# A linear attention with two feed-forward layers: a shorter bit algorithm for float64 weights, spread out phase by phase, and limb subtractions on VectorE

## The chip, the cores and the metric

The program runs on one core of a Trainium2 chip. Its engines work side by side, each through its own list of instructions in order: TensorE (PE), VectorE (DVE), ScalarE (ACT), GpSimd (POOL) and SyncE (SP), which issues the transfers. The metric is the device time in microseconds (us) of one execution, as the median of several runs; lower is better.

## What is computed

Three stages, float32 in and out, over 4 batches x 576 tokens (2304 in all), 8 heads of 64:

```python
q_p, k_p = phi(q * scale), phi(k * scale)      # phi: exp(x omega^T - |x|^2/2 - max), 128 features
num = q_p @ (k_p^T v);  den = q_p @ sum(k_p)   # linear attention, per batch and head
x = num / (den + 1e-6)                         # 2304 x 512
h = x @ moe_w_in;  g = relu(h) ** 2;  x = g @ moe_w_out      # 512 -> 2048 -> 512
h = x @ moe2_w_in; g = elu(h);        out = g @ moe2_w_out
```

The four weight matrices arrive as float64. The kernel makes float32 of them by operations on their bits.

## The kernel before

**Precision.** Every float32 operand of the large products is split into two limbs, high and low (`h`, `l`): ACT writes the high one with a cast, and a subtraction, the helper `minus` (line 74), leaves the low one. A product then is three matmuls (high x high, high x low, low x high) that accumulate in a PSUM bank.

**Attention.** The work is cut into 36 units: per batch four of k, four of q and one of the tokens left over. They pass through a hand-written list of stages (lines 516 to 519), one unit further per *tick*: load, square (POOL), transpose on PE with cast (ACT, `th`) and subtraction (DVE, `tl`), projection on PE (`pp`), maxima (DVE), exp (ACT), use on PE, division (DVE, `xs`), transpose again with limbs (`xh`, `xl`). `tc.manual_schedule()` keeps this order: what is issued first in a tick stands first in its engine's list. From tick 16 on, a tick also holds one or two products of the feed-forward layers.

**Feed-forward layers.** Per layer 16 chunks f of 128 columns of the hidden dimension, in 4 groups of 4. In a group the five token blocks (four of 512 tokens, a small one of 256) are worked on in turn, the small one second, but last in the last group. A *step* is a block and a chunk: `gemm1`, 12 matmuls, with the activation behind it (`r`, `gf`, its limbs `gh` and `gl`), and two steps later `gemm2`, 12 matmuls into `py`. After a block's fourth step DVE adds the banks to `ya` (lines 478 to 485). So PE alternates gemm1 of a step and gemm2 of the step two before; each is called a product below. All PSUM is a pool of 8 banks, all large data a pool of 93 pages.

**Weights.** A matrix chunk (a *part*, 64 in all) goes through three phases: `make_squares` (fetch, and a Square of the high words on ACT, tile `cm`), `make_floats` (four bit operations on DVE, tile `cv`), `make_limbs` (cast `wh` on ACT, subtraction `wl` on POOL). Three staging buffers (`st`) hold fetched chunks. `make(n)` takes one part each through all three phases, oldest first. It is called in each tick from 13 on for the first group's 8 parts, and after attention on every second product, up to 12 parts ahead of the number already used up.

Of the kernel before, what the change touches and what calls it, by code (L numbers as in the profile page):

```python
# [17 lines left out]
def linear_attention_two_ffn_kernel(  # L18
# [19 lines left out]
    C = S // P                    # whole token tiles of a batch  # L38
    L = S - C * P                 # tokens left over
    LH = 2                        # of the tokens left over, heads on top of each other on the partitions  # L40
    KD = DM // P
    NF = DFF // P
    GF = 4                        # f chunks of a group
    NG = NF // GF
    BLKS = [C * P] * B + [B * L]  # token blocks: the whole tiles of each batch, then what is left
    NB = len(BLKS)
    W = 512
    LOOK = 2                      # steps from a gemm1 to its gemm2
# [3 lines left out]
    # the square of the float32 that has a float64's high word for 2^-126 as its bits  # L52
    TINY = (1.125 * 2.0 ** -15) ** 2
# [5 lines left out]
    # nearly all data lives in pages of one size  # L59
# [19 lines left out]
    # x of each layer and block, d on the partitions: pages of limbs, one a chunk of d (two for the small block)  # L79
    xh, xl = {}, {}  # L80

    def x_pages(moe, i, c, name):
        """pages of chunk c, and their part for it"""
        per = W // BLKS[i]
        for d, s in ((xh, "h"), (xl, "l")):
            if (moe, i, c // per) not in d:
                d[moe, i, c // per] = page([per, BLKS[i]], f"x{s}{moe}_{i}_{c // per}", F32R)

# [26 lines left out]
    # Keeps sign and the exponent's top bit, drops the three exponent bits that float32 has not, and takes  # L115
    # three mantissa bits of the low word; what float32 holds no normal number for goes to zero.
    def make_squares(n):
# [3 lines left out]
        nc.scalar.activation(out=staged[p][1], in_=staged[p][0][:, :, 1].bitcast(F32), func=AF.Square)  # L121

    def make_floats(n):
# [4 lines left out]
        nc.vector.tensor_scalar(  # L128
            out=t, in0=hi, scalar1=3, scalar2=0x3FFFFFFF, op0=ALU.logical_shift_left, op1=ALU.bitwise_and
        )  # L130
        nc.vector.scalar_tensor_tensor(  # L131
            out=t, in0=hi, scalar=0xC0000000, in1=t, op0=ALU.bitwise_and, op1=ALU.bitwise_or
        )
# [3 lines left out]
        tf = t.bitcast(F32)  # L137
        nc.vector.scalar_tensor_tensor(out=tf, in0=m, scalar=TINY, in1=tf, op0=ALU.is_ge, op1=ALU.mult)  # L138
        staged[p] = tf
        fetch(n + 3)  # L140

    def make_limbs(n):
# [5 lines left out]
        minus(nc.gpsimd, l, tf, h)  # L148
        w_t[p] = h, l

    def make(n):
        """goes on with the parts before n, each one phase further"""
        n = min(n, len(parts))
        for f, c in ((make_limbs, 2), (make_floats, 1), (make_squares, 0)):
            if n_made[c] < (n if c == 0 else n_made[c - 1]):
                f(n_made[c])
# [8 lines left out]
    # A unit is [P, 4, 2, D]: four pairs of rows of D, each pair of one partition's tokens (or, of the tokens  # L165
    # left over, of two heads). A pair is transposed and projected as one, by a block diagonal omega^T.
# [43 lines left out]
    def load_v(u):  # L210
# [4 lines left out]
        if kind == "l":  # L215
            # of two heads on top of each other, each with zeros beside it
# [20 lines left out]
    def transposed(u):  # L237
        """x^T of a unit, scaled, in limbs; the sum over d of x^2"""
# [29 lines left out]
    def maxima(u):  # L268
# [9 lines left out]
        # max h = max(proj) - sq / 2;  h - max h = proj - sq / 2 - max h  # L278
# [3 lines left out]
    def featured(u):  # L282
        """exp(h - max h) of a unit, token by token"""
# [12 lines left out]
    def used(u):  # L296
        """phi(k)^T [v, 1] of two heads, or phi(q)^T of a unit"""
# [227 lines left out]
    with tc.manual_schedule():  # L525
        load(units[0])
        omega_limbs()
        for s in range(1, len(units) + DEPTH):
            for f, d in stages:
# [3 lines left out]
                elif f == "weights":  # L533
                    if s >= WEIGHTS:
                        make(2 * GF)
# [38 lines left out]
```

## Time and profile before

| | before |
|---|---|
| device time, median of 3 runs (lowest to highest) | 1016.61 us (1015.27 to 1016.76) |
| span of the profiled execution, first to last instruction | 1009.8 us |
| median of the runs above that span | 6.8 us |
| PE busy | 978.4 us, 97% |
| DVE busy | 637.0 us, 63% |
| ACT busy | 476.3 us, 47% |
| POOL busy | 391.8 us, 39% |
| mean granted TensorE clock | 0.992 of full speed (2.4 GHz) |

Attention fills the first quarter of the span, layer 1 (moe=0) the time up to about 600 us, layer 2 (moe=1) the rest. The busy share is an average over these: which engine is waited for is a question to each stretch. A busy time counts an instruction from its start to its modelled end; matmuls overlap, so their rate is read from the number that start in a stretch (x in the tables by stage).

### The profile page before, as it was taken

What the parts mean: (1) busy time and instruction counts of PE and PEld (TensorE: products, weight loads), DVE (VectorE), ACT (ScalarE), POOL (GpSimd) and SP (SyncE); (2) the same over time, 40 slices, a digit from 0 to 9 for tenths busy, and PEclk for the clock granted to TensorE, in tenths of its full rate; (3) what the DMA queues carried; (4) which work ended last, traced back from release to release, by engine and by line L of the source; (5) the groups of instructions that cost most, each with busy time, mean ns of one, the idle gap of its engine ahead of it and who ended that gap; (6) DMA issues with size and microseconds to landing.
All of it is one profiled execution on the core that took longest, in us unless ns stands there. A gap on an engine that the chain in (4) does not pass through costs nothing.

```text
span 1009.8 us, 14294 instructions
## 1 busy us (share of the span) xinstructions
PE 978.4 (97%) x5441; PEld 840.7 (83%) x5441; DVE 637.0 (63%) x1031; ACT 476.3 (47%) x1051; POOL 391.8 (39%) x359
## 2 busy tenths in 40 slices
PE   8977999999999999999999997999999999999998
PEld 7977899999888888888888886888788878888886
DVE  7899866654797249524962498339933993384333
ACT  6875565654443234322443354445454545454443
POOL 7345533321445225423464465224522443243221
PEclk9998999999999999999999999999999999999999
DMA  7333421200222002100210022002200230000211
GB/s 180 115 115 105 114 50 48 74 2 2 82 89 80 1 21 84 63 1 21 87 61 0 8 80 81 1 1 83 84 1 1 67 100 1 1 21 1 78 48 63
DMA packets 56469, 53.39 MB, mean 53 GB/s; under 512 B 25424, under 2 KB 50000, under 8 KB 56400
## 3 DMA queue, kind: packets, MB, share of 16 engines
q1 hardware_dynamic: 56240, 52.21, 17.0%
q8 instruction: 43, 0.70, 0.3%
q10 hardware_dynamic: 160, 0.26, 0.1%
q14 instruction: 26, 0.21, 0.1%
HBM read 47.74 MB, written 4.72 MB: 52 GB/s over the span
## 4 chain that ended last, share of the span: by engine, by line
PE 76%; DVE 19%; issue 2%; ACT 1%; DMA 1%; SPq 0%; POOL 0%; DVEq 0%; POOLq 0%; ACTq 0%
PE ph L419 33%; PE py L461 32%; DVE cv L134 4%; DVE cv L138 3%; DVE cv L131 3%; PE pn L345 2%; DVE cv L128 2%; DVE r L439 1%; DVE ya L485 1%; DVE gf L440 1%; PE pk2k L312 1%; PE pk3k L312 1%; PE pk0k L312 1%; PE pp2q L263 1%; PE pp3k L263 1%
## 5 line engine op out<-in xcount | busy, mean ns | idle before, releaser
L74 POOL TENSOR_TENSOR gl<-gf,gh 128x512 fp32r<-128x512 f32 (+1 forms) x171 | 195.0, 1141 | 569.0 <-ACT gh L441 241.3
L419 PE MATMUL ph<-xh,wh 128*128 128x512 f32 (+1 forms) x688 | 246.5, 358 | 5.5 <-DVE gf L440 5.5
L419 PE MATMUL ph<-xl,wh 128*128 128x512 f32 (+1 forms) x688 | 246.1, 358 | 0.0
L419 PE MATMUL ph<-xh,wl 128*128 128x512 f32 (+1 forms) x688 | 246.1, 358 | 0.0
L419 PEld LDWEIGHTS ph<-xh,wh 128*128 128x128 f32 x688 | 129.9, 189 | 27.8 <-DVE gf L440 6.8
L439 DVE SCALAR_TENSOR_TENSOR r<-r,t 128x512 f32<-128x512 f32 (+1 forms) x80 | 52.7, 658 | 158.8 <-ACT t L438 158.8
L432 DVE TENSOR_TENSOR gf<-r 128x512 f32<-128x512 f32 (+1 forms) x92 | 55.5, 604 | 151.7 <-ACT r L430 150.8
L419 PEld LDWEIGHTS ph<-xl,wh 128*128 128x128 f32 x688 | 129.7, 189 | 21.0
L419 PEld LDWEIGHTS ph<-xh,wl 128*128 128x128 f32 x688 | 129.7, 188 | 20.6
L430 ACT ACTIVATE r<-ph 128x512 f32<-128x512 f32 (+1 forms) x92 | 46.5, 506 | 211.6 <-PE ph L419 209.1
L461 PE MATMUL py<-gh,wh 128*128 128x512 f32 (+1 forms) x368 | 128.6, 349 | 0.0
L461 PE MATMUL py<-gl,wh 128*128 128x512 f32 (+1 forms) x368 | 127.0, 345 | 0.0
L461 PE MATMUL py<-gh,wl 128*128 128x512 f32 (+1 forms) x368 | 126.9, 345 | 0.0
L461 PE MATMUL py<-wh,gl 128*128 128x512 f32 x288 | 114.7, 398 | 2.4 <-POOL gl L74 2.4
L441 ACT CAST gh<-gf 128x512 fp32r<-128x512 f32 (+1 forms) x80 | 46.2, 578 | 148.8 <-DVE gf L440 148.8
L461 PE MATMUL py<-wh,gh 128*128 128x512 f32 x288 | 114.2, 396 | 1.3 <-ACT gh L441 1.3
L461 PE MATMUL py<-wl,gh 128*128 128x512 f32 x288 | 113.9, 395 | 0.0
L74 POOL TENSOR_TENSOR wl<-cv,wh 128x512 fp32r<-128x512 f32 x64 | 103.3, 1613 | 26.6 <-ACT wh L147 26.4
L134 DVE SCALAR_TENSOR_TENSOR cv<-st,cv 128x512 uint32<-128x512 uint32 x64 | 88.7, 1386 | 2.2
L461 PEld LDWEIGHTS py<-gh,wh 128*128 128x128 f32 x368 | 69.2, 188 | 9.5
L461 PEld LDWEIGHTS py<-gh,wl 128*128 128x128 f32 x368 | 69.3, 188 | 9.3
L461 PEld LDWEIGHTS py<-gl,wh 128*128 128x128 f32 x368 | 69.2, 188 | 9.3
(322 smaller groups left out, 1600.4 us busy)
## 6 DMA issues: line engine op xcount, KB each, us to landing
st<-in_moe_w_in_dram SPq DMA_DIRECT2D x32, 512.0 KB, 3.6
st<-in_moe_w_out_dram SPq DMA_DIRECT2D x32, 512.0 KB, 3.4
out_dram<-ya SPq DMA_DIRECT2D x16, 256.0 KB, 2.3
ld0k<-in_k_dram SPq DMA_DIRECT2D x4, 256.0 KB, 3.6
v0k<-in_v_dram SPq DMA_DIRECT2D x8, 128.0 KB, 4.2
ld0q<-in_q_dram SPq DMA_DIRECT2D x4, 256.0 KB, 3.8
ld1k<-in_k_dram SPq DMA_DIRECT2D x4, 256.0 KB, 4.9
v1k<-in_v_dram SPq DMA_DIRECT2D x8, 128.0 KB, 3.9
```

Source lines behind the costliest of these rows:

```text
L74: eng.tensor_tensor(out=out, in0=whole, in1=hi.bitcast(F32), op=ALU.subtract)
L128: nc.vector.tensor_scalar(out=t, in0=hi, scalar1=3, scalar2=0x3FFFFFFF, op0=ALU.logical_shift_left, op1=ALU.bitwise_and)
L131: nc.vector.scalar_tensor_tensor(out=t, in0=hi, scalar=0xC0000000, in1=t, op0=ALU.bitwise_and, op1=ALU.bitwise_or)
L134: nc.vector.scalar_tensor_tensor(out=t, in0=lo, scalar=29, in1=t, op0=ALU.logical_shift_right, op1=ALU.bitwise_or)
L138: nc.vector.scalar_tensor_tensor(out=tf, in0=m, scalar=TINY, in1=tf, op0=ALU.is_ge, op1=ALU.mult)
L312: nc.tensor.matmul(o, phs[h][:, c, :], st[u]["v"][:, h * C + c, :], start=False, stop=c == C - 1, skip_group_check=True,)
L419: nc.tensor.matmul(ph[:, :n], wt[:, cs], x_part(xt, moe, i, c)[:, n0:n1], start=(m == 0), stop=(m == 3 * KD - 1))
L430: nc.scalar.activation(out=r, in_=ph[:, :n], func=AF.Relu)
L432: nc.vector.tensor_tensor(out=gf, in0=r, in1=r, op=ALU.mult)
L439: nc.vector.scalar_tensor_tensor(out=r, in0=r, scalar=1.0, in1=t, op0=ALU.add, op1=ALU.mult)
L441: nc.scalar.copy(out=gh, in_=gf)
L461: nc.tensor.matmul(y, *((w[:, ts], a) if moe == 0 else (a[:, ts], w)), start=j == 0 and m == 0 and t % per == 0, stop=j == GF - 1 and m == ...
```

## The change

- The conversion's bit algorithm: ACT multiplies the high words, read as float32, by 2^-112 instead of squaring them; DVE then builds the float32 with one mask and two shift-and-or operations, three instructions instead of four.
- `make` takes the phases that it is to go on with. In attention one phase per tick from tick 2 on (a part per three ticks), after it one phase per product (a part per three products), instead of all three in each tick from 13 on and on every second product.
- Every `minus` runs on DVE: `wl` of the weights, `gl` of the activations, `xl` of layer 2's input, which ran on POOL.

```diff
-    def make_squares(n):
+    def make_rebiased(n):
         fetch(n + 1)
         p = parts[n]
         staged[p] = staged[p], page([W], "cm{}_{}_{}".format(*p))
-        nc.scalar.activation(out=staged[p][1], in_=staged[p][0][:, :, 1].bitcast(F32), func=AF.Square)
+        nc.scalar.activation(out=staged[p][1], in_=staged[p][0][:, :, 1].bitcast(F32), func=AF.Copy, scale=REBIAS)
 
     def make_floats(n):
...
-        nc.vector.tensor_scalar(
-            out=t, in0=hi, scalar1=3, scalar2=0x3FFFFFFF, op0=ALU.logical_shift_left, op1=ALU.bitwise_and
-        )
-        nc.vector.scalar_tensor_tensor(
-            out=t, in0=hi, scalar=0xC0000000, in1=t, op0=ALU.bitwise_and, op1=ALU.bitwise_or
-        )
+        nc.vector.tensor_scalar(out=t, in0=hi, scalar1=0x80000000, scalar2=None, op0=ALU.bitwise_and)
         nc.vector.scalar_tensor_tensor(
             out=t, in0=lo, scalar=29, in1=t, op0=ALU.logical_shift_right, op1=ALU.bitwise_or
         )
-        tf = t.bitcast(F32)
-        nc.vector.scalar_tensor_tensor(out=tf, in0=m, scalar=TINY, in1=tf, op0=ALU.is_ge, op1=ALU.mult)
-        staged[p] = tf
+        nc.vector.scalar_tensor_tensor(
+            out=t, in0=m.bitcast(U32), scalar=3, in1=t, op0=ALU.logical_shift_left, op1=ALU.bitwise_or
+        )
+        staged[p] = t.bitcast(F32)
         fetch(n + 3)
 
     def make_limbs(n):
...
         nc.scalar.copy(out=h, in_=tf)
-        minus(nc.gpsimd, l, tf, h)
+        minus(nc.vector, l, tf, h)
         w_t[p] = h, l
 
-    def make(n):
-        """goes on with the parts before n, each one phase further"""
+    def make(n, phases=(2, 1, 0)):
         n = min(n, len(parts))
-        for f, c in ((make_limbs, 2), (make_floats, 1), (make_squares, 0)):
+        for c in phases:
             if n_made[c] < (n if c == 0 else n_made[c - 1]):
-                f(n_made[c])
+                (make_rebiased, make_floats, make_limbs)[c](n_made[c])
                 n_made[c] += 1
...
-        minus(nc.vector if (moe, g, o, j) == steps[-1] else nc.gpsimd, gl, gf, gh)
+        minus(nc.vector, gl, gf, gh)
...
-                minus(nc.gpsimd, lo, ya, hi)
+                minus(nc.vector, lo, ya, hi)
...
-    WEIGHTS, TWO = 13, 25
+    WEIGHTS, TWO = 2, 25
...
                     if s >= WEIGHTS:
-                        make(2 * GF)
+                        make(2 * GF, ((s - WEIGHTS) % 3,))
...
         for n, s in enumerate(work):
-            if n % 2 == 0:
-                make(n_dead[0] + 12)
+            make(n_dead[0] + 12, (2 - n % 3,))
```

Three places show how the instructions move. The first is the start of ACT's list, ticks 1 to 4. `th0k`, `th0l` and `th0q` are the casts of the first three units, `cm_0_0` and `wh_0_0` belong to the first part of the weights, `st_0_0` is its staging buffer. Before:

```order
L249 ACT_TABLE_LOAD
L249 CAST th0k_114<-pt0k_109 128x512
L249 CAST th0l_136<-pt0l_131 128x512
L249 CAST th0q_172<-pt0q_167 128x512
L290 ACTIVATE ph0k_0_176<-pp0k_0_140,nb0k_157 128x128 x4
```

With the change:

```order
L122 ACT_TABLE_LOAD
L122 ACTIVATE cm_0_0_106<-st_0_0_104 128x512
L246 CAST th0k_118<-pt0k_113 128x512
L246 CAST th0l_148<-pt0l_143 128x512
L144 CAST wh_0_0_174<-cv_0_0_130 128x512
L246 CAST th0q_188<-pt0q_183 128x512
```

`cm_0_0`, which reads a fetched chunk of the weights, now stands ahead of the first unit's cast, and `wh_0_0` ahead of the third's.

The second is DVE's list at the turn to layer 2: `ya0_3_0` to `ya0_3_3` are the last block's sums of layer 1 (their limbs `xh1_3`, `xl1_3` are layer 2's input), `r1_0_0_0_2`, `gf` and `gl` belong to layer 2's third step, `wl1_3_0` is the low limb of the weights of its fourth. Before (`xl1_3`, `gl` and `wl1_3_0` are on POOL, `wl1_3_0` ahead of the four `xl1_3`):

```order
L440 TENSOR_TENSOR gf1_0_0_0_1_6664<-r1_0_0_0_1_6667,ph1_0_0_0_1_6651 128x512
L485 TENSOR_TENSOR ya0_3_0_4034<-py0_3_3_0_0_6526,ya0_3_0_4034 128x512
L485 TENSOR_TENSOR ya0_3_1_4036<-py0_3_3_0_1_6527,ya0_3_1_4036 128x512
L485 TENSOR_TENSOR ya0_3_2_4038<-py0_3_3_0_2_6528,ya0_3_2_4038 128x512
L485 TENSOR_TENSOR ya0_3_3_4040<-py0_3_3_0_3_6529,ya0_3_3_4040 128x512
L128 TENSOR_SCALAR cv1_4_0_6712<-st1_4_0_6597 128x512
L131 SCALAR_TENSOR_TENSOR cv1_4_0_6712<-st1_4_0_6597,cv1_4_0_6712 128x512
L134 SCALAR_TENSOR_TENSOR cv1_4_0_6712<-st1_4_0_6597,cv1_4_0_6712 128x512
L138 SCALAR_TENSOR_TENSOR cv1_4_0_6712<-cm1_4_0_6649,cv1_4_0_6712 128x512
L439 SCALAR_TENSOR_TENSOR r1_0_0_0_2_6737<-r1_0_0_0_2_6737,t1_0_0_0_2_6738 128x512
L440 TENSOR_TENSOR gf1_0_0_0_2_6734<-r1_0_0_0_2_6737,ph1_0_0_0_2_6721 128x512
```

With the change:

```order
L482 TENSOR_TENSOR ya0_3_0_4006<-py0_3_3_0_0_6487,ya0_3_0_4006 128x512
L74 TENSOR_TENSOR xl1_3_0_6636<-ya0_3_0_4006,xh1_3_0_6635 128x512
L482 TENSOR_TENSOR ya0_3_1_4008<-py0_3_3_0_1_6488,ya0_3_1_4008 128x512
L74 TENSOR_TENSOR xl1_3_1_6641<-ya0_3_1_4008,xh1_3_1_6640 128x512
L482 TENSOR_TENSOR ya0_3_2_4010<-py0_3_3_0_2_6489,ya0_3_2_4010 128x512
L74 TENSOR_TENSOR xl1_3_2_6646<-ya0_3_2_4010,xh1_3_2_6645 128x512
L482 TENSOR_TENSOR ya0_3_3_4012<-py0_3_3_0_3_6490,ya0_3_3_4012 128x512
L74 TENSOR_TENSOR xl1_3_3_6651<-ya0_3_3_4012,xh1_3_3_6650 128x512
L436 SCALAR_TENSOR_TENSOR r1_0_0_0_2_6672<-r1_0_0_0_2_6672,t1_0_0_0_2_6673 128x512
L437 TENSOR_TENSOR gf1_0_0_0_2_6669<-r1_0_0_0_2_6672,ph1_0_0_0_2_6656 128x512
L74 TENSOR_TENSOR gl1_0_0_0_2_6671<-gf1_0_0_0_2_6669,gh1_0_0_0_2_6670 128x512
L74 TENSOR_TENSOR wl1_3_0_6682<-cv1_3_0_6616,wh1_3_0_6681 128x512
```

Each `xl1_3` now stands between two `ya0_3` on DVE, and `wl1_3_0` comes behind all of them and behind the third step's `gl`; before, DVE was converting the next group's first part (`cv1_4_0`) there.

The third is DVE's list in layer 1's second group: `gf0_1_0_0_2` is of the step with block 0 and the third chunk, `wl0_6_1`, `cv0_7_0` and `wl0_7_0` are of the weights of the third and fourth chunk. Before:

```order
L128 TENSOR_SCALAR cv0_8_0_4232<-st0_8_0_4141 128x512
L131 SCALAR_TENSOR_TENSOR cv0_8_0_4232<-st0_8_0_4141,cv0_8_0_4232 128x512
L134 SCALAR_TENSOR_TENSOR cv0_8_0_4232<-st0_8_0_4141,cv0_8_0_4232 128x512
L138 SCALAR_TENSOR_TENSOR cv0_8_0_4232<-cm0_8_0_4189,cv0_8_0_4232 128x512
L432 TENSOR_TENSOR gf0_1_0_0_2_4254<-r0_1_0_0_2_4257 128x512
L128 TENSOR_SCALAR cv0_8_1_4282<-st0_8_1_4187 128x512
L131 SCALAR_TENSOR_TENSOR cv0_8_1_4282<-st0_8_1_4187,cv0_8_1_4282 128x512
L134 SCALAR_TENSOR_TENSOR cv0_8_1_4282<-st0_8_1_4187,cv0_8_1_4282 128x512
L138 SCALAR_TENSOR_TENSOR cv0_8_1_4282<-cm0_8_1_4239,cv0_8_1_4282 128x512
L432 TENSOR_TENSOR gf0_1_0_0_3_4304<-r0_1_0_0_3_4307 128x512
```

With the change:

```order
L429 TENSOR_TENSOR gf0_1_0_0_2_4201<-r0_1_0_0_2_4204 128x512
L74 TENSOR_TENSOR gl0_1_0_0_2_4203<-gf0_1_0_0_2_4201,gh0_1_0_0_2_4202 128x512
L74 TENSOR_TENSOR wl0_6_1_4210<-cv0_6_1_4164,wh0_6_1_4209 128x512
L129 TENSOR_SCALAR cv0_7_0_4229<-st0_7_0_4102 128x512
L130 SCALAR_TENSOR_TENSOR cv0_7_0_4229<-st0_7_0_4102,cv0_7_0_4229 128x512
L133 SCALAR_TENSOR_TENSOR cv0_7_0_4229<-cm0_7_0_4186,cv0_7_0_4229 128x512
L74 TENSOR_TENSOR wl0_7_0_4236<-cv0_7_0_4229,wh0_7_0_4235 128x512
L429 TENSOR_TENSOR gf0_1_0_0_3_4252<-r0_1_0_0_3_4255 128x512
L74 TENSOR_TENSOR gl0_1_0_0_3_4254<-gf0_1_0_0_3_4252,gh0_1_0_0_3_4253 128x512
```

Where DVE converted the third group's first part (`cv0_8_0`, `cv0_8_1`) around this step, it now converts `cv0_7_0`, and its `wl0_7_0` follows at once: the next product on PE after the running one, gemm1 of the fourth chunk, reads it.

## Rows read from the trace of the kernel before

**Rows 1.** The page: busy time and share of PE, and its 40 slices.

```profile
PE 978.4 (97%) x5441; PEld 840.7 (83%) x5441; DVE 637.0 (63%) x1031; ACT 476.3 (47%) x1051; POOL 391.8 (39%) x359
PE   8977999999999999999999997999999999999998
```

**Rows 2.** The chain of waits: start, length, engine, tile, line, count.

```profile
251.94 2.78 PE ph L419 x12
```

**Rows 3.** By stage: length, busy PE, PEld, DVE, ACT, POOL (instructions), clock, DMA, GB/s.

```profile
0.00:25.00 25.00, 20.31 (x142) 18.72 (x142) 19.71 (x38) 15.30 (x44) 18.27 (x32) 1.00 0.70 179
15.00:50.00 35.00, 35.00 (x313) 34.68 (x312) 31.64 (x78) 28.90 (x94) 18.18 (x27) 1.00 0.56 154
25.00:50.00 25.00, 25.00 (x226) 24.81 (x225) 21.85 (x61) 20.00 (x66) 8.57 (x15) 1.00 0.39 119
50.00:111.00 61.00, 48.55 (x375) 46.28 (x373) 58.81 (x110) 39.43 (x113) 29.66 (x32) 0.92 0.34 101
```

**Rows 4.** The same table for tile cv alone: DVE, ACT, POOL.

```profile
50.00:111.00 61.00, 30.28 (x32) 5.01 (x8) 10.12 (x8) 0.92 0.34 101
```

**Rows 5.** PE's longest wait, 40 to 130 us: total, times, longest.

```profile
PE pn L345 <- DVE tl1q L74: 3.6, 2, 2.4
```

**Rows 6.** The table by stage, three windows; matmuls of one kind, 600 to 630.

```profile
600.00:630.00 30.00, 24.94 (x119) 19.75 (x118) 27.82 (x32) 14.46 (x32) 19.04 (x14) 0.94 0.22 71
710.00:730.00 20.00, 17.92 (x98) 14.69 (x97) 19.49 (x26) 9.13 (x20) 9.78 (x7) 1.00 0.33 106
815.00:835.00 20.00, 17.92 (x100) 14.74 (x99) 19.38 (x26) 9.93 (x22) 11.08 (x8) 1.00 0.35 106
...
L419 PE MATMUL ph<-xh,wl 128*128 128x256 f32 x16 | 4.6, 289 | 0.0
```

**Rows 7.** PE's waits, 595 to 630 us.

```profile
PE py L461 <- POOL gl L74: 1.9, 3, 0.8
PE ph L419 <- DVE gf L440: 1.8, 1, 1.8
```

**Rows 8.** Conversion and limbs by line: shortest, median, longest in ns.

```profile
L128 DVE TENSOR_SCALAR cv<-st x64: 410/420/1269, 50.4 to 906.3; 128x512 uint32<-128x512 uint32 x64
L134 DVE SCALAR_TENSOR_TENSOR cv<-st,cv x64: 691/1666/1696, 51.6 to 907.5; 128x512 uint32<-128x512 uint32 x64
...
L74 POOL TENSOR_TENSOR wl<-cv,wh x64: 1264/1737/1766, 55.3 to 914.2; 128x512 fp32r<-128x512 f32 x64
```

**Rows 9.** Timeline, 607 to 612 us: start, length, engine, line.

```profile
607.72 0.69 DVE L440 TENSOR_TENSOR gf<-r,ph 128x512 f32<-128x512 f32 x1
609.14 1.47 POOL L74 TENSOR_TENSOR gl<-gf,gh 128x512 fp32r<-128x512 f32 x1 [2.00 <-ACT gh L441]
609.51 1.65 DVE L134 SCALAR_TENSOR_TENSOR cv<-st,cv 128x512 uint32<-128x512 uint32 x1
610.58 1.75 POOL L74 TENSOR_TENSOR wl<-cv,wh 128x512 fp32r<-128x512 f32 x1
```

**Rows 10.** Timeline of the start: ACT's first cast, SP's third kind of load.

```profile
5.04 0.58 ACT L249 CAST th0k<-pt0k 128x512 fp32r<-128x512 f32 x1 [3.02 <-PE pt0k L246]
5.73 0.62 SPq L203 DMA_DIRECT2D ld0q<-in_q_dram  x1
```

**Rows 11.** Transfers of layer 1's input weights: size, us to landing.

```profile
st<-in_moe_w_in_dram SPq DMA_DIRECT2D x32, 512.0 KB, 3.6
```

**Rows 12.** Instructions by line: total, mean ns, idle before.

```profile
L121 ACT ACTIVATE cm<-st 128x512 f32<-128x512 f32 x64 | 42.7, 667 | 0.0
L334 DVE TENSOR_TENSOR xs<-pn,rd 128x256 f32<-128x256 f32 x32 | 13.6, 424 | 1.2
```

**Rows 13.** Timeline of the turn to layer 2, 597 to 603 us.

```profile
597.22 2.47 DVE L485 TENSOR_TENSOR ya<-py,ya 128x512 f32<-128x512 f32 x4
597.93 2.47 ACT L492 CAST xh<-ya 128x512 fp32r<-128x512 f32 x4
602.55 0.62 ACT L438 ACTIVATE t<-gf 128x512 f32<-128x512 f32 x1
```

More of the change, by code (lines that the diff above doesn't have):

```diff
@@ L51, in linear_attention_two_ffn_kernel @@
     EPS = 1e-6 * M
-    TINY = (1.125 * 2.0 ** -15) ** 2
+    REBIAS = 2.0 ** -112
     assert LH * L == P and C == 4 and H == 4 * LH and 2 * NP * (C * P) == W * H and NP == KD
```

## The prediction

> **What bounds the kernel now.** I read the page first: PE is busy for 978.4 of 1009.8 us, and its slices show 9 or more nearly throughout, with gaps in the first fifth and around 600 us [rows 1]. So the time is PE's list of matmuls plus the places where PE idles or runs slow. Next the chain of waits: a product of twelve 512-column matmuls takes 2.78 us [rows 2]. The feed-forward layers hold 8 groups x 36 such products, 801 us, which no edit here touches. Attention and all stalls share the remaining 209 us.
>
> Then the table by stage [rows 3]. From 25 to 50 us PE is busy throughout and starts 226 matmuls, 9.04 per us. From 50 to 111 us it starts 375; at that rate they need 41.5 us, so PE loses 19.5 us there. It idles for 12.5 of them, the rest is matmuls at a granted clock of 0.92 on average. DVE is busy for 58.81 of the 61 us, 30.28 of them for the weight conversion, tile cv [rows 4]: in ticks 13 to 21 the eight parts of the first group pass through DVE one per tick, and PE's longest wait there is for tl, DVE's attention work behind them [rows 5]. That is the first loss.
>
> The second lies in the feed-forward layers. PE's slices are full from 250 to 590 us [rows 1]; it idles in three windows, 600 to 630, 710 to 730 and 815 to 835 us, 9.2 us together [rows 6]. There the 256-column block of layer 2 (moe=1) is worked on. In the first window PE starts 119 matmuls, 48 of 256 columns (three groups of x16 [rows 6]) and 71 of 512: at 0.116 and 0.232 us 22.0 us, so 8.0 are lost, with the clock at 0.94. With the idle time of the other two that is 12. PE waits there for DVE's gf (L440), which releases a PSUM bank, and for gl from POOL [rows 7].
>
> **The parts and their prices.** A conversion on DVE now is four instructions, 30.28 / 8 = 3.8 us in that stage [rows 4], but their lengths are not fixed: L134 lies between 691 and 1696 ns with a median of 1666 [rows 8]. The timeline tells why: L134 starts at 609.51 while POOL's gl runs from 609.14 to 610.61, and ends at 611.16, 0.55 us behind it; the next POOL instruction then takes 1.75 us, against 1.26 at its fastest [rows 9, 8]. After the change one tensor_scalar and two scalar_tensor_tensor remain, in the forms of L128 and L134 [rows 8]: at the minima 0.41 + 0.69 + 0.69 = 1.8 us. The limb subtraction comes to them from POOL at 0.69, as L440, also two inputs of 512 elements [rows 9]. So 2.5 us a part where POOL is idle, as it now is in the feed-forward layers. In attention POOL keeps its squares: the four instructions now take 3.8 instead of 2.5 beside a POOL that is busy for 29.66 of 61 us [rows 3], so 2.5 to 3.8 there; I take 2.9, since the squares fill less of the time than squares and limbs.
>
> The Trainium skill (SBUF — State Buffer, "Who interferes with whom") says that a VectorE instruction with two SBUF inputs, and one in a two-port mode, excludes a GpSimd instruction that reads SBUF for that one's whole length. The overlap above agrees: 1.65 us instead of 0.69, and POOL's 1.75 instead of 1.26. The rule speaks against the change as long as squares run; by it alone a part in attention would cost the upper end, which is rival 2.
>
> First term, ticks 13 to 21: the burst goes, -19.5 us.
>
> Second term, the start. ACT gets cm of the first part ahead of th of the first unit (the order of ACT). SP can issue its load only behind v of unit 0, at 5.73 us, where ld0q goes out now [rows 10]; such a load lands after 3.6 us [rows 11], cm takes 0.67 [rows 12]: th starts near 10.0 us instead of 5.04, and tl, pp and all behind go with it. PE is busy in every us from 15 to 50 [rows 3], so nothing gives this back: +5 us. Bounds: 0, if PE, which idles for 4.7 of its first 25 us [rows 3], only waits less later; 8, if cv in tick 3 and three loads of 512 KB among the first q and k loads add to it.
>
> Third term, ticks 3 to 13: DVE is busy for 31.64 of the 35 us up to 50 [rows 3] and gets three whole parts, 8.7 us: 40.3, or 5.3 over. DVE may first fall behind PE by a part of a tick, 2 us; +3 (0 to 8).
>
> Fourth term, ticks 14 to 25: without cv 28.5 us of DVE's 58.81 remain; four parts add 11.6 and five gl of 256 columns 2.1 (0.42 each, as L334 of that size [rows 12]): 42.2 beside PE's 41.5, in uneven ticks: +1.5 (0 to 5).
>
> Fifth term, the feed-forward layers. A group's conversion spreads over 24 products instead of 16, so in three groups the last part comes out hardly ahead of its use; DVE does everything in order, behind what waits for ACT.
> - The turn to layer 2. The order of DVE puts ahead of wl1_3_0: r, gf, gl of the second step, cv1_3_0, four times ya and xl, then r, gf, gl of the third step. Count from the end of layer 1's last product. The second step's gemm1 ended at -2.8. Three ACTIVATEs take 1.8, r, gf and gl 0.7 each, gh and the other casts 0.62 [rows 9, 13], so gl is out at +1.7, cv at 3.5. Each ya needs its cast xh on ACT before xl: 0.62 + 0.62 + 0.69 and the hand-overs, 2.0, four times 8.0: 11.5. Behind the last xh (10.8) come the third step's three ACTIVATEs, 12.6, r, gf and gh, 14.6, then gl and ACT's wh, 15.3, and wl, 16.0. PE wants wl1_3_0 after two products and two matmuls, at 6.0. It waits 10 us. Today POOL does xl and wl and PE passes here without a wait. Behind such a stop ACT and DVE are abreast again, so the small block after it costs nothing.
> - Layer 1's second group. Floats and limbs of its last input part, cv0_7_0 and wl0_7_0, stand right ahead of the gemm1 that uses them, behind gl and wl0_6_1 of the product before the last. From the end of that gemm1: r 0.6, gf and gl 1.4, wl 0.7, cv 1.8, wh 0.6, wl 0.7, 5.8 against the 2.78 + 0.46 that PE needs until it asks: 2.6 us. The part after it, wl0_7_1, has no product ahead either: some 1.5. Together 4.
> - The last group of layer 2: wl1_15_0 has one product ahead; counted as at the turn, with four ya alone (2.47 [rows 13]) in place of the 8.0, it is 3.3 us late. In the other groups two or three products lie between, which is enough.
> - The small blocks of the second and third group of layer 2: DVE's conversion falls from 4.5 to 1.7 us a step; 1.5 left of 4.
>
> With the 1.8 us that a clock of 0.94 costs in the window at 600 us, to be expected behind a longer stop as well: 10 + 4 + 3.3 + 1.5 + 1.8 = 20.6 in place of 12: about +8. Bounds: -1, if the 16.0 at the turn shrinks to 10 and the rest is half; +13, if DVE comes to each of these places 2 us behind.
>
> ACT swaps a Square for a scaled Copy of the same shape: nothing. Later weight loads stay three parts, over 20 us, ahead of their use, which hides their 3.6 us.
>
> Sum: -19.5 + 5 + 3 + 1.5 + 8 = -2 on a span of 1009.8: 1007.8. The runs' median is 6.8 us above that span, for what lies around it and doesn't change: 1014.6, say 1014.
>
> **Rivals.**
> 1. The start is absorbed and attention is free: terms two to four together 4 us, the fifth +2: 1016.6 - 13.5 = 1003. For it: PE has 4.7 us of idle time at the start, and the three minima of conversion are short. Against: ACT, DVE and PE hang on one another there, a unit or two apart.
> 2. Slower, by the squares: attention stays bound by DVE, from tick 3 instead of 13. At 3.8 us a part, the seven parts of terms three and four cost 6 more than I took, DVE's lag adds 2: 5 + 12.5 with the fifth at 8 is +6, so 1022. It makes the kernel slower from 3.2 us a part. For it: DVE has only 3.4 us idle from 15 to 50. Against: POOL, with squares alone, is busy for only 8.57 us of the 25 from 25 to 50 [rows 3].
> 3. Slower, DVE and ACT become one loop in layer 2: in order on DVE gl waits for gh, in order on ACT the next step's ACTIVATEs wait until gh is out. With no overlap a step needs 1.8 + 2.8 (r, gf, gh, gl) + 1.7 of conversion = 6.3 us for PE's 5.57: over 40 steps with conversions +28, about 1042. Against: gl and conversion, 2.4 us, can run beside the ACTIVATEs.
>
> **How the numbers follow.** The forecast, 1014 (own range 1007 to 1019): 0.43. Rival 1, below 1007: 0.26. Rival 2, 1019 to 1028: 0.23. Rival 3: 0.08. Within 0.2% (2 us, about what a measurement tells from no change) lies 0.18, of the forecast's own range; faster is rival 1 and the half of the forecast below 1014.6, 0.48; slower the rest, 0.34. The range, 1000 to 1026, leaves out rival 3, the far end of rival 1 and the end of rival 2.
>
> **What will show it.** In the feed-forward stages cv at 0.42, 0.69 and 0.69 us; th of unit 0 near 10 us; PE full from 60 to 110 us, but short of it before 50; one PE wait of 8 us or more for wh or wl at layer 2's first fourth step, smaller ones near 265 and 890 us; none for a bank in the small blocks. I am wrong if PE is full again by 15 us (rival 1), if cv and wl take over 3.5 us a part up to 110 us with PE idle (rival 2), if PE waits for gl in the large blocks (rival 3), or if the turn to layer 2 shows no wait for wh or wl.

## The result, and the profile after

| | before | with the change |
|---|---|---|
| median of 4 runs (lowest to highest), us | 1016.37 (1015.27 to 1016.76) | 1024.0 (1022.75 to 1025.16) |
| ratio to before, 95% interval | | 1.0082 (1.0063 to 1.0102) |
| span of the profiled execution, us | 1009.8 | 1021.2 |

The kernel became 7.6 us slower; the forecast was 2 us faster. The time lies in the range, the direction was wrong.

The page after, busy times and PE's 40 slices:

```profile
PE 980.6 (96%) x5441; PEld 842.3 (82%) x5441; DVE 649.9 (64%) x1220; ACT 475.5 (47%) x1051; POOL 71.1 (7%) x106
...
PE   6999999999989999999999987999999999998998
```

The gap in the first fifth is gone but for its ends; new ones show in the twelfth slice (near 300 us) and the 37th (near 925 us), and the one at 600 us is as deep as before. DVE is busy 13 us longer than before, POOL has its squares alone: 71.1 us instead of 391.8. DVE's busy share (64%) does not show what follows; where its work stands in the list does.

By stage, in the columns of [rows 3]:

```profile
0.00:25.00 25.00, 15.27 (x88) 13.40 (x89) 16.00 (x32) 10.97 (x29) 14.32 (x27) 1.00 0.81 227
25.00:50.00 25.00, 22.71 (x187) 22.14 (x186) 23.76 (x55) 19.22 (x61) 15.58 (x23) 0.93 0.48 132
50.00:111.00 61.00, 59.05 (x510) 57.12 (x509) 54.53 (x135) 45.41 (x141) 19.49 (x27) 1.00 0.36 103
111.00:140.00 29.00, 24.83 (x195) 23.34 (x194) 21.30 (x51) 16.92 (x51) 6.26 (x7) 0.88 0.14 40
600.00:630.00 30.00, 19.83 (x86) 15.82 (x85) 17.13 (x27) 12.64 (x23) 0.00 (x0) 0.83 0.11 35
710.00:730.00 20.00, 20.00 (x94) 16.48 (x93) 15.75 (x26) 11.44 (x21) 0.00 (x0) 1.00 0.21 71
```

Against [rows 3]: from 50 to 111 us PE starts 510 matmuls instead of 375, at the full granted clock, and idles for 1.9 us instead of 12.5. But the first 25 us start 88 instead of 142 and the next 25 start 187 instead of 226. Against [rows 6]: the window at 710 is full now (the small blocks lie some 10 us later, and PE loses next to nothing there either: 660-900 in the table below); from 600 to 630 us PE idles for 10.2 us instead of 5.1, at a mean granted clock of 0.83 instead of 0.94.

PE's waits in the five places where it loses time, 0 to 40, 110 to 140, 285 to 325, 590 to 630 and 905 to 935 us: the longest of those that the kernel before does not have (who waits, for whom; total, times, longest).

```profile
PE pp0k L260 <- ACT th0k L246: 4.5, 1, 4.5
PE pp0q L260 <- DVE tl0q L74: 1.8, 1, 1.8
```

```profile
PE py L458 <- ACT wh L144: 2.3, 1, 2.3
PE px L373 <- DVE tl2q L74: 1.5, 1, 1.5
```

```profile
PE ph L416 <- ACT wh L144: 2.7, 1, 2.7
PE py L458 <- ACT wh L144: 1.4, 1, 1.4
```

```profile
PE ph L416 <- ACT wh L144: 10.2, 1, 10.2
```

```profile
PE ph L416 <- ACT wh L144: 3.0, 1, 3.0
```

In four of the five the longest is for wh, the high limb of a weight part: the part comes out too late for the product that reads it.

To compare kernels I count, for every matmul, the time to the next start beyond the usual one (lower quartile) of its form and size, and add this up by stretch. The count holds idle time and slow clock alike. Grouping the matmuls in another way moves a single figure by up to 1.5 us. Some 5 us of "rest" and 2.3 us at 660-900 stand in kernels in which PE waits for nothing there; below this is called the bare rest.

| lost by PE, us | 0-40 | 40-110 | 110-140 | 280-340 | 590-660 | 660-900 | 900- | rest | all |
|---|---|---|---|---|---|---|---|---|---|
| before | 5.5 | 20.3 | 1.0 | 0.8 | 8.7 | 7.9 | 1.1 | 5.3 | 50.6 |
| the change | 15.6 | 4.9 | 7.7 | 7.1 | 12.5 | 2.5 | 6.3 | 5.0 | 61.6 |
| a: old pace after attention | 15.1 | 5.4 | 8.0 | 0.6 | 6.4 | 2.3 | 0.9 | 5.1 | 43.8 |
| b: old pace in attention | 5.7 | 19.8 | 2.6 | 7.3 | 13.5 | 2.5 | 7.1 | 5.4 | 63.9 |
| c: subtractions on POOL | 12.9 | 6.3 | 6.1 | 10.7 | 11.6 | 2.4 | 7.6 | 5.4 | 63.0 |
| d: both old paces | 6.1 | 18.2 | 1.0 | 0.5 | 6.2 | 2.3 | 1.0 | 5.2 | 40.5 |
| e: a part per two ticks from 5 | 14.2 | 10.8 | 1.2 | 0.5 | 6.4 | 2.3 | 1.0 | 5.5 | 41.9 |
| f: first chunk fetched first | 14.2 | 5.0 | 8.7 | 0.4 | 6.4 | 2.4 | 0.8 | 5.1 | 43.0 |
| g: bit algorithm alone | 5.8 | 12.9 | 0.8 | 0.6 | 3.1 | 2.3 | 0.8 | 5.1 | 31.4 |
| h: subtractions on DVE alone | 6.6 | 21.6 | 6.4 | 0.6 | 13.6 | 16.3 | 2.0 | 5.6 | 72.7 |
| i: parts up to 14 ahead | 17.2 | 4.9 | 7.8 | 7.2 | 8.0 | 2.6 | 1.1 | 5.3 | 54.1 |
| j: g, and gl on DVE | 6.5 | 16.3 | 1.8 | 0.6 | 5.8 | 5.4 | 1.0 | 5.0 | 42.4 |

The two traces differ by 11.0 in this count and by 11.4 in their spans, the medians by 7.6. In the profiled runs since, whose time is known, 1.8 us lie around the span (1023.02 and 1021.2), not the 6.8 that the prediction adds (to both kernels alike): the traced execution of before was some 5 us shorter than the median of its kernel. So a difference between single traces can be off by about 5 us, here by 3 to 4; the comparisons below go by the medians, and the places by losses that several runs share.

### The profile page after: what moved, and what is told of

It reads as the page before. It is cut to its first block, busy times and chain, and to the rows that moved or that the text cites. A ratio compares the mean times of both kernels' runs of the same rounds, so it can differ in the third digit from the quotient of the medians.

```text
span 1021.2 us, 13964 instructions
## 1 busy us (share of the span) xinstructions
PE 980.6 (96%) x5441; PEld 842.3 (82%) x5441; DVE 649.9 (64%) x1220; ACT 475.5 (47%) x1051; POOL 71.1 (7%) x106
## 4 chain that ended last, share of the span: by engine, by line
PE 90%; DVE 6%; ACT 2%; issue 0%; DMA 0%; SPq 0%; POOL 0%; DVEq 0%; ACTq 0%; POOLq 0%
PE ph L416 39%; PE py L458 38%; PE pn L342 3%; DVE cv L130 1%; DVE cv L133 1%; PE pk2k L309 1%; PE pk3k L309 1%; PE pk1k L309 1%; PE pp2q L260 1%; DVE ya L482 1%; PE pp3k L260 1%; PE pp3q L260 1%; PE px L373 1%; PE pk0k L309 1%; DMA st<-in_moe_w_in_dram 0%
## 5 line engine op out<-in xcount | busy, mean ns | idle before, releaser
L416 PEld LDWEIGHTS ph<-xh,wh 128*128 128x128 f32 x688 | 130.2, 189 | 39.0 <-ACT wh L144 17.2
L74 DVE TENSOR_TENSOR gl<-gf,gh 128x512 fp32r<-128x512 f32 (+1 forms) x172 | 104.2, 606 | 61.5 <-ACT gh L438 51.1
L429 DVE TENSOR_TENSOR gf<-r 128x512 f32<-128x512 f32 (+1 forms) x92 | 52.9, 575 | 138.0 <-ACT r L427 137.7
L433 ACT ACTIVATE gf<-ph 128x512 f32<-128x512 f32 (+1 forms) x80 | 44.2, 553 | 76.8 <-PE ph L416 76.8
L482 DVE TENSOR_TENSOR ya<-py,ya 128x512 f32<-128x512 f32 x108 | 68.7, 682 | 1.4 <-PE py L458 1.4
```

Source lines behind the costliest of these rows:

```text
L74: eng.tensor_tensor(out=out, in0=whole, in1=hi.bitcast(F32), op=ALU.subtract)
L416: nc.tensor.matmul(ph[:, :n], wt[:, cs], x_part(xt, moe, i, c)[:, n0:n1], start=(m == 0), stop=(m == 3 * KD - 1))
L429: nc.vector.tensor_tensor(out=gf, in0=r, in1=r, op=ALU.mult)
L433: nc.scalar.activation(out=gf, in_=ph[:, :n], func=AF.Relu, scale=-1.0)
L482: nc.vector.tensor_tensor(out=ya, in0=yv, in1=ya, op=ALU.add)
```

## The experiments

Two theories to begin with. The first: the pace loses the time, by single parts that come out with no product ahead of their use, and by the early start. The second: the subtractions on DVE lose it, because DVE works in order and waits for ACT's casts, whatever the pace. Each run is compared with the kernel before, on the same chip.

**a. The old pace after attention.**

```diff
-            make(n_dead[0] + 12, (2 - n % 3,))
+            if n % 2 == 0:
+                make(n_dead[0] + 12)
```

> The changed kernel, but after attention the weights are made as before: every second product, all three phases. Theory 1 (the loss comes from the pace, which brings single parts out with no product ahead of their use): the waits of PE for wh near 300, 608 and 915 us go, 2.7 + 1.4, 10.2 and 3.0 us in its profile, and with them the matmuls at the lower clock behind each; by the starts of matmuls these places cost 24 us. DVE then does 2.5 + 2.8 us in a step of 5.57, so the small blocks may cost 1 to 3: 1002, 1000 to 1005. Theory 2 (the limb subtractions themselves keep DVE too busy and in line behind ACT, whatever the pace): the turn to layer 2 stays a wait of 8 us or more and the small blocks stall too: 1015 to 1024.

Measured: 1004.36, ratio 0.9912 (0.9896 to 0.9928). The waits for wh after attention are gone (280-340 and 900- lose under 1 us each), at the turn 6.4 are left, in which PE waits for gh and for a bank:

```profile
PE py L458 <- ACT gh L438: 2.4, 2, 2.0
PE ph L416 <- DVE gf L437: 2.1, 1, 2.1
```

The ratios of the change and of a differ by 0.017, 17 us, and the same conversions and subtractions run in both. The first theory holds for the layers: the pace alone costs 17 us there.

**b. The old pace in attention.**

```diff
-    WEIGHTS, TWO = 2, 25
+    WEIGHTS, TWO = 13, 25
-                        make(2 * GF, ((s - WEIGHTS) % 3,))
+                        make(2 * GF)
```

> The changed kernel, but in attention the weights are made as before: from tick 13 on, all three phases in each tick. Theory 1 (pace): th of unit 0 is at 5 us again, which gives back 10 us of the first 40; the wait for wh at 128 us goes, 6; in exchange eight parts of 2.5 to 3.3 us stand in ticks 13 to 21 again, against 41.5 us of PE and 30.6 of other DVE work, which costs 9 to 15 in place of today's 5. Sum: 1024 - 10 - 6 + 4 to 10 = 1012 to 1018, 1015. Theory 2 (the cost in attention is the conversion and its limbs on DVE, not where they stand): the start and the end give nothing, the burst costs 15 more: 1030 or above.

Measured: 1022.97, 1.0083 (1.0053 to 1.0112), no better than the change. The start and the end are mended as the first theory says (5.7 and 2.6), but ticks 13 to 21 lose 19.8, as much as before and more than the 9 to 15 I allowed. Tile cv from 50 to 111 us, DVE and ACT, then tile wl, PE, PEld and DVE:

```profile
50.00:111.00 61.00, 25.19 (x31) 5.01 (x8) 0.90 0.45 128
```

```profile
50.00:111.00 61.00, 6.99 (x24) 4.83 (x24) 6.36 (x7) 0.90 0.45 128
```

The 31 DVE instructions of the first line are 24 of conversion and the seven subtractions wl, which read cv. So eight conversions take 25.19 - 6.36 = 18.83 us, 2.4 each, and a subtraction takes 0.91: 3.3 a part, the upper end of the 2.5 to 3.3 I allowed. DVE's work for the weights fell, from 30.28 us [rows 4] to some 26 for eight whole parts, and the stretch loses as much as before. So DVE's sum alone does not explain this loss. PE's longest wait there is 3.1 us for tl1k, which stands in DVE's list behind a wl that waits for ACT's wh, and behind a conversion (66.94 to 70.18 us); that this order is the cause of the whole is argued, not shown.

**c. All three subtractions back on GpSimd**, new algorithm and pace kept.

```diff
-        minus(nc.vector, l, tf, h)
+        minus(nc.gpsimd, l, tf, h)
-        minus(nc.vector, gl, gf, gh)
+        minus(nc.vector if (moe, g, o, j) == steps[-1] else nc.gpsimd, gl, gf, gh)
-                minus(nc.vector, lo, ya, hi)
+                minus(nc.gpsimd, lo, ya, hi)
```

> The changed kernel with the three subtractions (wl, gl, xl) back on GpSimd, new bit algorithm and new pace kept. Theory 1 (pace): the late parts stay late; at the turn to layer 2 POOL has xl four times (6.2 us), gl and wl in one list, so wl1_3_0 comes 6 to 9 us late instead of 10; the small blocks lose 2 to 4 us again, since DVE and POOL exclude each other; attention changes little. 1020 to 1030, 1024. Theory 2 (DVE's subtractions): with them gone the waits for wh shrink to half, the turn first: 1010 or below.

Measured: 1025.04, 1.0127 (1.0098 to 1.0155). The places are those of the change, the wait at the turn a little shorter:

```profile
PE ph L416 <- ACT wh L144: 6.8, 1, 6.8
PE ph L416 <- POOL wl L74: 1.5, 1, 1.5
```

The second theory falls for this pace: late parts are late on either engine, and with the subtractions on GpSimd the kernel is not faster than the change but if anything 4 to 5 us slower (1.0127 against 1.0082; the intervals just meet). What I expected for the small blocks was wrong: they lose only the bare rest.

**d. Both old paces.** The edits of a and b together.

> The changed kernel with both old paces: only the bit algorithm and the engine of the subtractions are new against the kernel before. Theory 1 (pace): the gains and losses of the two kernels with one old pace add up, 1024 - 22 - 9 = 993, 988 to 998, which is 23 below the kernel before: 12 from the small blocks, the rest from shorter conversions in attention. Theory 2: 1015 to 1030, not below the kernel before.

Measured: 1001.65, 0.9885 (0.9865 to 0.9904). Better than a, but 12 us short of the sum I expected, because b gave nothing of its own. The whole change of pace costs 1.0082 - 0.9885, 20 us: 17 after attention, 3 in it, where the 13 gained at 40-110 (a 5.4, d 18.2) go back at the start and the end (23.1 against 7.1).

**e. One part per two ticks from tick 5**, on a.

```diff
-    WEIGHTS, TWO = 2, 25
+    WEIGHTS, TWO = 5, 25
-                        make(2 * GF, ((s - WEIGHTS) % 3,))
+                        make(2 * GF, ((2, 0), (1,))[(s - WEIGHTS) % 2])
```

> The changed kernel with the old pace after attention (every second product), and in attention one part per two ticks from tick 5 on (cast and limbs with the next part's rescaling, then floats) instead of one per three ticks from tick 2. Theory 1 (the start costs because ACT and DVE get the first part ahead of the first units, the end because the last part has no product ahead of its use): against the run with the old pace after attention alone (8.4 us below the kernel before, of the same chip), the first 40 us lose 6 instead of 15, the wait for wh near 128 us goes with its 6.5, and ticks 13 to 21 lose 5 to 9 instead of 5, since more parts fall there: 18 to 24 below the kernel before, 22. Theory 2 (any conversion on DVE during attention costs its length): nothing is gained, since the same eight parts pass through DVE: 6 to 10 below.

Measured: 1003.04, 0.988 (0.9859 to 0.99). Half right: the end is mended (1.2), as in d, so the part without a product ahead was its cause. The start isn't (14.2). What ACT and PE wait for, 0 to 30 us:

```profile
ACT cm L122 <- DMA st<-in_moe_w_in_dram: 4.9, 1, 4.9
```

```profile
PE pk0k L302 <- issue: 4.4, 1, 4.4
```

Tick 5 is still too early for the chunk: cm waits for it at the head of ACT's list until 18.36 us, ahead of the exp for the unit that pk0k reads, and PE then waits as long as in the change (4.4 and 4.5 us).

**f. The first chunk fetched ahead of everything**, on a.

```diff
     with tc.manual_schedule():
+        fetch(1)
         load(units[0])
```

> The changed kernel with the old pace after attention, and the fetch of the first weight chunk issued ahead of the first unit's load instead of behind v of unit 0; the order on ACT stays. Theory 1 (th of unit 0 waits in line on ACT behind cm, and cm for that chunk): the chunk lands near 5 us, the first unit's load 1 to 3 us later than today, th starts at 6 to 7 us instead of 11, and the start loses 10 to 12 instead of 15: 3 to 5 us below the run without this. Theory 2 (the start costs by DVE's conversion in ticks 3 and 6 and by the extra loads' share of the transfers): no change, within 2 us.

Measured: 1006.38, 0.9906 (0.9881 to 0.9931), no change against a. The first theory's step came true: cm runs at 5.26 and th of unit 0 at 7.54 instead of 10.98. The time didn't follow: the loads of the units are late instead.

```profile
5.26 0.66 ACT L122 ACTIVATE cm<-st 128x512 f32<-128x512 f32 x1 [3.25 <-DMA st<-in_moe_w_in_dram]
7.54 0.59 ACT L246 CAST th0k<-pt0k 128x512 fp32r<-128x512 f32 x1 [1.62 <-PE pt0k L243]
```

```profile
PE pt0k L243 <- DMA ld0k<-in_k_dram: 7.2, 2, 4.1
```

So taking ACT's wait for the chunk away gains nothing: PE waits for the first units' loads in its place, 3.08 us for the first and 4.12 for the next k unit, which is issued right behind two more chunks. That the four chunks of 512 KB among these loads delay them is likely by this order, but no run separates it.

**g. The bit algorithm alone, and h. the subtractions alone**, on the kernel before: g has the change's `make_rebiased` and `make_floats` and nothing else, h its three `minus(nc.vector, ...)`.

> The kernel before with the new bit algorithm alone (three instead of four DVE instructions; old paces, subtractions on GpSimd). The run with both (new algorithm, subtractions on VectorE, old paces) was 11 below the kernel before. If DVE's length per part in the small blocks decides, this takes the conversion from 4.4 to 3 us there and a quarter off it in ticks 13 to 21: 5 to 10 below. If the subtractions on GpSimd, through the exclusion of DVE, are the cause: 0 to 3 below.

> The kernel before with the subtractions on VectorE alone (old bit algorithm, old paces). By the exclusion: conversions of 2.5 us without GpSimd beside them plus 0.7 for wl and 0.7 for gl, 3.9 a step in layer 2 against 4.4 and 1.7 of GpSimd today; 2 to 6 below, but 590 to 660 us stays as it is, since xl and ya alternate on DVE there. If the algorithm alone made the gain of 11: 0, or up to 5 above, since a part costs DVE 0.7 more in ticks 13 to 21.

Measured: g 993.04, 0.9782 (0.9762 to 0.9802); h 1031.99, 1.0163 (1.0134 to 1.0192). Both outside what I expected, to opposite sides. In g ticks 13 to 21 lose 12.9 instead of 20.3, the turn 3.1 instead of 8.7, the small blocks 2.3 instead of 7.9, the bare rest. In h the small blocks lose 16.3. g and c differ in the pace alone, and it costs 35 us there (1.0127 - 0.9782), more than the 20 that it costs with the subtractions on DVE. One small step of h, DVE, ACT and PE:

```profile
740.54 0.69 DVE L74 TENSOR_TENSOR wl<-cv,wh 128x512 fp32r<-128x512 f32 x1
...
743.06 0.69 DVE L138 SCALAR_TENSOR_TENSOR cv<-cm,cv 128x512 f32<-128x512 f32 x1
...
744.19 0.42 DVE L440 TENSOR_TENSOR gf<-r,ph 128x256 f32<-128x256 f32 x1
744.64 0.40 ACT L441 CAST gh<-gf 128x256 fp32r<-128x256 f32 x1 [3.09 <-DVE gf L440]
744.66 0.58 PE L419 MATMUL ph<-xh,wh 128*128 128x256 f32 x1 [2.96 <-DVE gf L440]
745.08 0.43 DVE L74 TENSOR_TENSOR gl<-gf,gh 128x256 fp32r<-128x256 f32 x1 [0.47 <-ACT gh L441]
```

wl, four instructions of conversion, r, gf, the wait for gh, gl: 5.06 us from one gl (740.02) to the next, all in DVE's one list, though no instruction is longer than 0.69. POOL has nothing to do here, as the change intends, and yet the step is longer than in the kernel before, where it takes 4.69 us from one gf (723.72) to the next with conversion instructions of up to 1.66 us beside POOL. In g it takes 4.10 (706.93 to 711.03). PE waits 2.96 us for gf.

**i. Parts up to 14 ahead**, the change's pace kept.

```diff
-            make(n_dead[0] + 12, (2 - n % 3,))
+            make(n_dead[0] + 14, (2 - n % 3,))
```

> The changed kernel, but after attention the parts may run 14 ahead of those used up instead of 12; the pace stays one part per three products. In the order of DVE wl1_3_0 now stands ahead of the four ya and xl at the turn to layer 2, and wl1_15_0 well ahead of the third step of the last group; wl0_7_0 stands where it stood, right ahead of its use. Theory 1 (single parts with too few products ahead of their use): the 10.2 us wait at the turn becomes the small block's waits of the run with the old pace, 6 lost instead of 12.5, the 3.0 near 915 us goes with its 6, the 2.7 + 1.4 near 300 us stay: 10 to 12 below the changed kernel, 1 to 4 below the kernel before. Theory 2 (DVE is too busy after attention at this pace, wherever the parts stand): all three waits stay, within 3 of the changed kernel.

Measured: 1014.0, 0.9989 (0.9971 to 1.0006), 9 us below the change by the ratios, just short of the 10 to 12 I expected. Place by place as the first theory says: 900- from 6.3 to 1.1, the turn from 12.5 to 8.0, 280-340 unmoved at 7.2. Between the two kernels only the position of parts in the lists differs. That shows the late parts as the cause of the waits at the turn and in the last group; the wait near 300 us, whose parts stand where they stood, agrees.

**j. The algorithm, with gl on DVE**, on g.

```diff
-        minus(nc.vector if (moe, g, o, j) == steps[-1] else nc.gpsimd, gl, gf, gh)
+        minus(nc.vector, gl, gf, gh)
```

> The new bit algorithm alone (22 below the kernel before), with gl on VectorE; wl and xl stay on GpSimd, old paces. By the places where the run with all three subtractions on VectorE lost more (5 in ticks 13 to 21, where wl is the most of it; 3 at the turn, where xl stands in line), gl costs nothing: within 2 of the algorithm alone, 20 to 24 below the kernel before. If gl, which waits for gh on ACT in DVE's list, is what costs: 10 to 16 below.

Measured: 1003.16, 0.9886 (0.9858 to 0.9913). A miss: gl alone costs 10 us against g, as much as all three subtractions in d (0.9885). So wl and xl on DVE cost nothing more in sum. The places differ, though: j loses 5.4 in the small blocks and d the bare rest of 2.3, d loses 18.2 at 40-110 and j 16.3. PE's longest wait after 40 us:

```profile
PE ph L415 <- DVE gf L436: 5.1, 3, 2.4
```

gf, which frees the bank, stands behind the gl of the step before and the conversion in DVE's list; from one gf to the next a small step takes 4.54 us (717.24 to 721.78), against the 4.10 of g.

**k. Two more paces on g**: one part per two ticks from tick 8, and two parts in three ticks from tick 10.

```diff
-    WEIGHTS, TWO = 13, 25
+    WEIGHTS, TWO = 8, 25
-                        make(2 * GF)
+                        make(2 * GF, ((2, 0), (1,))[(s - WEIGHTS) % 2])
```

```diff
-    WEIGHTS, TWO = 13, 25
+    WEIGHTS, TWO = 10, 25
-                    if s >= WEIGHTS:
+                    if s >= WEIGHTS and (s - WEIGHTS) % 3 != 2:
```

> The new bit algorithm alone, and in attention one part per two ticks from tick 8 on instead of one per tick from 13; subtractions on GpSimd, old pace afterwards. Theory 1 (the burst in ticks 13 to 21 still costs 13 by the starts of matmuls; spread out and begun when the loads are ahead it costs 5 to 7): 6 to 9 below the algorithm alone, 28 to 31 below the kernel before. Rival: the chunks' loads fall among the first units' loads as in the runs that began at ticks 2 and 5, and the first 40 us lose 4 to 8 more: within 3 of the algorithm alone.

> As the run with one part per two ticks from tick 8, but two parts in three ticks from tick 10 on. Less spread, later loads: the start loses nothing, ticks 13 to 21 lose 9 instead of 13: 3 to 6 below the algorithm alone.

Measured: 991.64, 0.9771 (0.9739 to 0.9804), and 993.33, 0.9788 (0.976 to 0.9816). Neither can be told from g: from tick 8 the start loses 9.0 instead of 5.8 and 40-110 still 11.0, from tick 10 it is 6.5 and 12.2. The best kernel of this study is the kernel before with the bit algorithm alone, 2.2% below it, with or without the spread.

## Why the prediction was wrong

By the table of losses, the forecast against what each stretch did. The last row comes from two traces; by the medians the change costs 7.6, so some 4 us of it belong to the traced executions, and the forecast missed by 9.6:

| | forecast | measured |
|---|---|---|
| start (second term, 0-40) | +5 | +10.1 |
| ticks 11 to 22 (first, third and fourth term, 40-110; the third begins at tick 3) | -15 | -15.4 |
| end of attention (110-140) | none | +6.7 |
| feed-forward (fifth term) | +8 | +9.9 |
| sum | -2 | +11.3 |

**The second term failed by its size.** Its mechanism came true. The change, ACT, PE and DVE:

```profile
10.42 0.66 ACT L122 ACTIVATE cm<-st 128x512 f32<-128x512 f32 x1 [8.40 <-DMA st<-in_moe_w_in_dram]
10.98 0.57 ACT L246 CAST th0k<-pt0k 128x512 fp32r<-128x512 f32 x1
...
13.99 0.41 PE L260 MATMUL pp0k<-oml,th0k 128*128 128x256 f32 x1
14.20 0.41 PE L260 MATMUL pp0k<-omh,th0k 128*128 128x256 f32 x1
...
24.42 1.11 DVE L130 SCALAR_TENSOR_TENSOR cv<-st,cv 128x512 uint32<-128x512 uint32 x1
25.57 1.41 DVE L133 SCALAR_TENSOR_TENSOR cv<-cm,cv 128x512 uint32<-128x512 uint32 x1
...
27.96 0.38 PE L260 MATMUL pp0q<-omh,tl0q 128*128 128x256 f32 x1 [1.81 <-DVE tl0q L74]
```

The second k unit's pk0k, in the kernel before and in the change:

```profile
23.91 0.39 PE L305 MATMUL pk0k<-v0l,ph0l 128*128 128x130 f32 x2
```

```profile
33.68 0.38 PE L302 MATMUL pk0k<-v0l,ph0l 128*128 128x130 f32 x2
```

th starts at 10.98 behind cm, forecast 10.0. I took the shift alone, and it came as forecast: PE's first pp0k starts at 11.61 instead of 6.55, the first pp0q at 18.58 instead of 13.43. (That PE starts its 256-column matmuls 0.21 us apart until 18 us, instead of 0.12 as later, adds nothing: the kernel before does so from 7.5 to 11 us.) But the delay grows to 9.8 us by the second pk0k, 33.68 instead of 23.91. PE waits 0.86 us ahead of the first pk0k. Then the second conversion, 2.93 us beside POOL's squares, stands ahead of tl0q; PE waits 1.81 us, and behind that stop the mean granted clock from 28 to 32 us is 0.57. I had 8 as a bound, with less than this in mind: the first conversion and the loads. The second conversion belongs to the third term, DVE falling behind from tick 3 on, and no run tells the two terms apart.

**A place was left out.** The last part of the first group, wl0_3_1, gets its limbs in tick 25 and is read in tick 25. I looked for such parts after attention, found three, and gave attention an average of DVE's load instead, so this place stands at nothing in the sum. wh came at 129.48, PE had waited 2.35 us and then worked from 130 to 133 us at a granted clock of 0.50; the 1.5 us for tl2q just before stand behind the same part's conversion (121.62 to 124.6 us). The runs d and e, in which the part has products ahead of it, lose 1.0 and 1.2 there.

**The first, third and fourth term together came out right**, and the 0.4 us are in part luck. The burst went, and the parts cost DVE what I took: 11.20 us for four from 50 to 111 us, 2.8 each, forecast 2.9 (conversions shorter than taken, 1.8, subtractions longer, 1.0). But the third term, +3, runs from tick 3 to 13, most of it before 40 us. Counted with the start it makes 8 against 10.1 there, and -18 against -15.4 here.

**The fifth term was right in its parts, short at two places.** (The times I gave for the smaller waits, 265 and 890 us, were 35 us early.) The turn, counted by hand as a wait of 10 us:

```profile
606.82 0.68 DVE L482 TENSOR_TENSOR ya<-py,ya 128x512 f32<-128x512 f32 x1
607.53 0.62 ACT L489 CAST xh<-ya 128x512 fp32r<-128x512 f32 x1 [3.15 <-DVE ya L482]
608.18 0.69 DVE L74 TENSOR_TENSOR xl<-ya,xh 128x512 fp32r<-128x512 f32 x1 [0.69 <-ACT xh L489]
...
617.79 0.62 ACT L438 CAST gh<-gf 128x512 fp32r<-128x512 f32 x1 [1.48 <-DVE gf L437]
618.32 0.61 ACT L144 CAST wh<-cv 128x512 fp32r<-128x512 f32 x1
...
618.98 0.79 PE L416 MATMUL ph<-xh,wh 128*128 128x512 f32 x1 [10.17 <-ACT wh L144]
...
619.58 0.63 PE L416 MATMUL ph<-xl,wh 128*128 128x512 f32 x1
620.00 0.63 PE L416 MATMUL ph<-xh,wl 128*128 128x512 f32 x1
```

ya, xh and xl take 1.97 us each time (606.82 to 608.79 for the first, by the start of the next ya), the next step's ACTIVATEs start behind the last xh (614.55), then r, gf, gh, wh: PE waits 10.17 us. The matmuls behind the stop start 0.42 us apart instead of 0.23 until 622; that is the 1.8 of clock I had added. Near 300 and 925 us I added none: waits of 2.7 + 1.4 and 3.0 us, forecast 2.6 + 1.5 and 3.3, cost 6.3 and 5.2 more than before by the starts. The small blocks lose the bare rest instead of the 1.5 kept.

**Rivals.** The second (slower by POOL's squares, 1022) is nearest in time, and its mechanism did not happen. Tile cv from 50 to 111 us in the change, DVE and ACT, then tile wl, PE, PEld and DVE:

```profile
50.00:111.00 61.00, 11.20 (x16) 2.54 (x4) 1.00 0.36 103
```

```profile
50.00:111.00 61.00, 7.57 (x27) 5.20 (x28) 3.99 (x4) 1.00 0.36 103
```

The 16 are twelve instructions of conversion and four wl, which read cv: four parts in 11.20 us, 2.8 a part, below the 3.2 from which that rival makes the kernel slower, and PE idles for only 1.9 us there. The first rival did not happen either: the start was not absorbed. Nor did the third: PE waits for no gl in the large blocks.

**What the Trainium skill said** (SBUF — State Buffer, "Who interferes with whom"), that a DVE instruction with two SBUF inputs and a GpSimd instruction that reads SBUF exclude each other, the traces agree with: in the change, where POOL has no work after attention, L133 has a median of 692 ns, where L134 had 1666 in the kernel before. What doesn't follow from it is that work should leave POOL for DVE: in h POOL is idle in the feed-forward layers, and h is slower by 1.6%.

What stays open: why gl alone costs 10 us on DVE in j, as much as all three subtractions in d. Against g, j loses 3 more each at 40-110, at the turn and in the small blocks. For the small blocks I can name gf's place behind gl; for the other two I can't say what weighs more, gl in DVE's list or POOL's wl beside DVE's conversion. Open as well is why b and d lose as much at 40-110 as the kernel before, or nearly, with less work on DVE, and how the delay at the start divides between the chunks' loads and the second conversion.

## What to carry to other kernels

When work is spread thinner, list for every piece how many steps lie between its issue and its first use, over the whole program and in every stage; here the pieces with none or one made the stops, and the average load of the engine did not show them. Price each stop of PE at the wait, and give it as an upper bound the matmuls at half rate that may follow. A change of three parts is three changes: here, taken in this order, one gained 22 us (g), the second lost 11 of them (d) and the third 20 more.

## What the runs showed of the hardware that was not expected

Behind some stops PE works at a granted clock of 0.50, the lower of its two levels: from 130 to 133 us and from 618 to 622 us, behind stops of 2.35 and 10.17 us; from 28 to 32 us the mean is 0.57, behind one of 1.81. Where this happens, a short stop costs in clock much as a long one: near 300 us 6.3 more is lost than before, for 4.1 of waits, near 925 us 5.2 for 3.0. It does not happen behind every stop: in run a PE waits 1.82 us in the same place for the same tile, and the granted clock from 28 to 32 us is 1.00. What decides between the two no run here shows. The change, then run a:

```profile
11.00:18.00 7.00, 6.25 (x27) 1.00 1.00 289
28.00:32.00 4.00, 4.00 (x21) 0.57 0.98 246
130.00:133.00 3.00, 2.69 (x11) 0.50 0.00 0
618.00:622.00 4.00, 3.02 (x7) 0.50 0.02 5
```

```profile
27.68 0.39 PE L260 MATMUL pp0q<-omh,tl0q 128*128 128x256 f32 x1 [1.82 <-DVE tl0q L74]
```

```profile
28.00:32.00 4.00, 3.62 (x32) 1.00 0.83 214
```

At the start the table's clock column reads 1.00 for 11 to 18 us, while the distances between matmuls (0.21 us) are those of the 0.50 stretches; there only the distances show it. The kernel before has the same from 7 to 11 us:

```profile
7.00:11.00 4.00, 3.96 (x19) 1.00 0.41 107
```
